# Loading v and k of the first four chunks from ScalarE's DMA queue in a retention kernel with two MLPs

## The chip, the core and the metric

The kernel runs on one core of a Trainium2 chip. TensorE (PE) multiplies matrices, VectorE (DVE), ScalarE (ACT) and GpSimd (POOL) work on elements, and SyncE (SP) issues transfers. A transfer between HBM and SBUF is issued as one instruction by an engine's sequencer and carried out by the core's 16 DMA engines. The metric is the device time of one execution in microseconds (us); lower is better.

## What is computed

A multi-head retention layer (2 sequences, 8 heads, 768 steps, head size 64), then two MLPs of 512 to 2048 to 512 on its 1536 tokens, all in float32.

```python
for t in range(S):
    state = gamma[None, :, None, None] * state + np.einsum('bhd,bhe->bhde', k[:, :, t], v[:, :, t])
    y[:, :, t] = scale * np.einsum('bhd,bhde->bhe', q[:, :, t], state)
x = y, tokens by 512
h = x @ w_in;  x = (h * tanh(log1p(exp(h)))) @ w_out      # first MLP
h = x @ w_in2; out = (h * cos(h)) @ w_out2                # second MLP
```

## The kernel before

The time steps are cut into chunks of 128, so there are 12 chunks (`NCHK`), numbered g = 0 to 11; chunks 0 to 5 are the first sequence, 6 to 11 the second. A chunk's inputs are one array of 128 rows by 2048 float32. Columns 0 to 1023 hold q and k transposed (below "qk"); columns 1024 to 2047 hold v and k in natural order (below "vk"). Each half is one transfer of 512 KB (`att_load`, L281, the issue itself is L294), so the 12 chunks are 24 transfers. `chunk_loads` (L584) plans them, in the order qk0, vk0, qk1, vk1 and so on. Everything is issued on SP: first the constants (`few`, L758, 146 KB), then the chunks, with four halves of weight tiles (`raw`, L211) among them.

What is done with a chunk, in the order in which PE meets it (`chunk_scores`, `chunk_inter`, `chunk_update`, `chunk_out`):

- scores (L325, below "s"), which need qk; DVE multiplies them by a mask (L332, tile `p`)
- inter (L370, "i"), which needs the state of the chunk before (tile `st`, from ACT at L353 or DVE) and `qd`, q times a decay, made by POOL from qk (L313, L316); not for chunks 0 and 6
- update (L341, "u"), which needs vk and `vd`, v times a decay, made from vk by ACT for chunks 1, 2, 4, 7 and 9 (L308) and by POOL for chunks 0, 3, 6, 8 and 10 (L305); not for chunks 5 and 11
- out (L381, "y"), which needs `p` and vk; ACT (L395) and DVE (L398) then store the result as x in a high and a low part

PE's order is s0, some multiplications of zeros (L787), s1, u0, y0, s2, i1, u1, y1, s3, i2, u2, y2, and so on: the scores of a chunk always stand ahead of the rest of the chunk before. After chunk 11 the two MLPs run as float32 products split in three terms (L428 and L451), for the remaining 525 us.

The order of the instructions comes from `Plan`: every step is entered with an engine, an estimated cost and what it needs, a list scheduler sets one order of all steps, and they are recorded in that order. Each engine runs its own in that order and waits on semaphores for the others. Transfers take eight semaphores (DMAHW0 to DMAHW7) in turn, in recorded order; a transfer whose semaphore was used by an earlier one is issued only after that earlier one has landed. So at most eight transfers are under way at a time.

Of the kernel before, what the change touches and what calls it, by code (L numbers as in the profile page):

```python
# [31 lines left out]
NCHK = B * NCH  # L32
IN_WO = (5, 6, 7)
IN_G = (8, 9)
H_ATT = {(0, 0, 0): "s", (0, 1, 0): "h0", (0, 0, 1): "y", (0, 1, 1): "h0"}
VD_ACT = (1, 2, 4, 7, 9)
ST_ACT = (3, 4, 6, 7, 8, 9)
# [34 lines left out]
class Plan:  # L72
# [15 lines left out]
    def op(self, engine, cost, fn, *args, needs=(), uses=(), new=None):  # L88
        n = len(self.ops)
        uses = list(uses)  # L90
        before = set(needs)
        reuse = None
        if new is not None:
            key, bufs, *tag = new
            line = self.lines.setdefault(tag[0] if tag else key[0], [])
            if line:
                before.add(self.owner[line[-1]])
            if len(line) >= bufs:
                reuse = line[-bufs]
            line.append(key)  # L100
            self.owner[key] = n
            uses.append(key)
        for key in uses:
            if self.owner.get(key, n) != n:
                before.add(self.owner[key])
            self.users.setdefault(key, set()).add(n)
        if engine in self.given:
            before |= {self.last[engine]} if engine in self.last else set()
            self.last[engine] = n
        att = fn.__name__.startswith("att") or fn.__name__ in ("start_up", "zeros", "load_consts")  # L110
        self.ops.append(dict(engine=engine, cost=cost, fn=fn, args=args, before=before, reuse=reuse, att=att))
        return n
# [64 lines left out]
def retention_two_mlps(ctx: ExitStack, tc: tile.TileContext, qkv, w1i, w1o, w2i, w2o, consts, out):  # L177
    nc = tc.nc
# [14 lines left out]
    spare = const_p.tile([128, 1], F32, name="spare")  # L193
# [87 lines left out]
    def att_load(g, lo, hi, eng=nc.sync):  # L281
        if not att:
            t = x_p.tile([128, 2, KD, BLK], F32R, tag="x", name="qkv")
            for n in range(2):
                att[n] = t[:, n].rearrange("p a b -> p (a b)").bitcast(F32)
        elif g in IN_WO and g not in att:
            t = wo_p.tile([128, 2, 2, 512], F32R, tag="wo", name="qkv")
            att[g] = t.rearrange("p a b c -> p (a b c)").bitcast(F32)
        elif g in IN_G and g not in att:
            t = g_p.tile([128, 2, 2, BLK], F32R, tag="g", name="qkv")  # L290
            att[g] = t.rearrange("p a b c -> p (a b c)").bitcast(F32)
        elif g not in att:
            att[g] = att_p.tile([128, 2048], F32, tag="qkv", name="qkv", bufs=3)
        eng.dma_start(out=att[g][:, lo:hi], in_=qkv[g, :, lo:hi])  # L294
# [117 lines left out]
    def h_tag(k):  # L412
        if k in H_ATT:
            return H_ATT[k]
        return "h0" if k[0] == 0 and k[1] < 2 else f"h{1 - k[2]}"
# [115 lines left out]
    plan = Plan()  # L531
    op = plan.op
    at = {"gs": []}
# [47 lines left out]
    def chunk(g):  # L581
        return ("qkv", max(g, 1))

    def chunk_loads(g, cuts, queue=nc.sync):  # L584
        key = chunk(g)
        for lo, hi in zip(cuts, cuts[1:]):
            n = op(
                "SP", (hi - lo) * (0.00142 if g < 3 else 0.00122), att_load, g, lo, hi, queue,
                uses=[key], new=None if key in plan.owner else (key, 3, "x" if g < 2 else "wo" if g in IN_WO else "g" if g in IN_G else "qkv"),
            )  # L590
            for part, last in (("qk", 1024), ("v", 1536), ("k", 2048)):
                if lo < last and hi > last - 512:
                    at.setdefault((part, g), []).append(n)

    def chunk_pre(g):
        c = g % NCH
        key = chunk(g)
        on_act = g in VD_ACT
        if c + 1 < NCH:
            at["vd", g] = [  # L600
                op(
                    *(("ACT", 0.98) if on_act else ("POOL", 1.15)), att_vd, g, part, needs=at["v", g] + at["dec"],
                    new=None if part else (("vd", g), 2), uses=[key, ("vd", g)],
                )
                for part in range(2 if on_act else 1)
            ]
        if c > 0:
            name, cost, eng = ("DVE", 0.72, nc.vector) if g in QD_DVE else ("POOL", 1.95, nc.gpsimd)
            at["qd", g] = op(
                name, cost, att_qd, g, eng, needs=at["qk", g] + at["decq"], new=(("qd", g), 2), uses=[key]  # L610
            )

    def nothing():
        pass
# [42 lines left out]
    def tile_in(m, G, j, f, parts=range(KD), only=None):  # L657
# [9 lines left out]
        for kks, terms in calls:  # L667
# [5 lines left out]
            )  # L673
            if H_ATT.get(k, "h0") != "h0":
                plan.ops[last]["att"] = True
# [12 lines left out]
        elif m == 0:  # L688
            last = op("ACT", 1.06, mish, k, needs=[last, table], new=(t, 3), uses=[h])
            plan.ops[last]["att"] = H_ATT.get(k, "h0") != "h0"  # L690
        else:
# [68 lines left out]
    def few(lo, n):  # L760
        return few_t[0][:, lo : lo + n]
# [34 lines left out]
    at["close"] = op(None, 0.0, close)  # L796
    op("PE", 5.5, start_up)
    load = op("SP", 0.4, load_consts, new=("few", 3, "g"))
    cuts = (0, 1024, 2048)
    for g in range(7):  # L800
        chunk_loads(g, cuts)
    weight(("i", 0, 0), lambda: [chunk_loads(g, cuts) for g in (7, 8, 9)])
    for g in (10, 11):
        chunk_loads(g, cuts)
# [16 lines left out]
    def products(n):  # L821
        for i, f, *rest in deal.get(n, ()):
            tile_in(*steps[i], f, *rest)

    chunk_pre(0)
    chunk_scores(0)
    op("PE", 1.1, zeros, 10, "u")
    for n in range(NCHK):
        if n + 1 < NCHK:
            chunk_pre(n + 1)  # L830
            chunk_scores(n + 1)
        chunk_inter(n)
        chunk_update(n)
        chunk_out(n)
        products(n)
        for it in later.get(n, ()):
            weight(it)
    def hold(n, *first):
        plan.ops[n]["before"] |= set(first)

    i00, i01 = ("i", 0, 0), ("i", 0, 1)
    for n, what, ns, it in (
        (6, "clamp", 0, i00), (7, "sign", 0, i00), (11, "dve low", 0, i00),
        (9, "clamp", 1, i00), (11, "dve low", 1, i00),
    ):
        hold(at[what, it, ns], at["p", n])
    hold(at["sign", i00, 1], at["xl", 9])
    hold(at["act", i00, 0], at["xh", 4])
    hold(at["act", i00, 1], at["xh", 6])
    hold(at["high", i00, 1], at["st", 10])  # L850
# [84 lines left out]
```

## Time and profile before

| what | value |
|---|---|
| median of 3 runs | 572.44 us |
| lowest and highest | 571.8 and 572.52 us |
| the profiled execution's own time | 573.28 us |
| its span, first to last instruction | 571.5 us |
| PE busy | 565.8 us, 99% of the span |
| granted PE clock | full throughout the span |
| bytes moved by transfers | 49.91 MB |

The span is the stretch that the trace shows; 1.8 us of the profiled execution lie around it. Times below count from the span's start. A row of the timeline gives start, length, engine, line, operation, output and input tiles, and in square brackets how long the engine had been idle and what released it. PEld is PE's weight load, SPq the sequencer of SP.

### The profile page before, as it was taken

What the parts mean: (1) busy time and instruction counts of PE and PEld (TensorE: products, weight loads), DVE (VectorE), ACT (ScalarE), POOL (GpSimd) and SP (SyncE); (2) the same over time, 40 slices, a digit from 0 to 9 for tenths busy, and PEclk for the clock granted to TensorE, in tenths of its full rate; (3) what the DMA queues carried; (4) which work ended last, traced back from release to release, by engine and by line L of the source; (5) the groups of instructions that cost most, each with busy time, mean ns of one, the idle gap of its engine ahead of it and who ended that gap; (6) DMA issues with size and microseconds to landing.
All of it is one profiled execution on the core that took longest, in us unless ns stands there. A gap on an engine that the chain in (4) does not pass through costs nothing.

```text
span 571.5 us, 7260 instructions
## 1 busy us (share of the span) xinstructions
PE 565.8 (99%) x3054; PEld 468.4 (82%) x3054; DVE 382.6 (67%) x416; ACT 230.1 (40%) x284; POOL 97.5 (17%) x74
## 2 busy tenths in 40 slices
PE   8999999999999999999999999999999999999997
PEld 6888888888888888888888888888888888888886
DVE  5779889662375427653487985898498894765462
ACT  3574543422303303214326465465345354354240
POOL 6680001111110301111101111032010312010000
PEclk9999999999999999999999999999999999999999
DMA  8982254422032200412021030304004010000113
GB/s 297 413 335 75 75 210 158 147 75 73 1 131 91 73 1 0 148 73 75 0 75 73 26 123 1 138 10 147 1 0 148 32 41 2 1 1 1 73 38 110
DMA packets 14721, 49.91 MB, mean 87 GB/s; under 512 B 1632, under 2 KB 2016, under 8 KB 14688
## 3 DMA queue, kind: packets, MB, share of 16 engines
q1 hardware_dynamic: 14688, 49.44, 23.4%
q8 instruction: 24, 0.39, 0.3%
q14 instruction: 9, 0.07, 0.0%
HBM read 46.29 MB, written 3.15 MB: 86 GB/s over the span
## 4 chain that ended last, share of the span: by engine, by line
PE 94%; DMA 4%; SPq 1%; ACT 0%; issue 0%; DVE 0%; ACTq 0%
PE ps_h L428 46%; PE ps_o L451 46%; DMA qkv<-qkv_dram 4%; SPq L294 1%; PE ps_y L381 1%; PE ps_y L370 1%; PE ps_s L325 1%; PE ps_u L341 0%; ACT vd L308 0%; ACT x L395 0%; DVE acc L517 0%; SPq L758 0%; ACT st L353 0%; ACTq L308 0%
## 5 line engine op out<-in xcount | busy, mean ns | idle before, releaser
L428 PE MATMUL ps_h<-x,wi 128*128 128x512 f32 x1152 | 264.8, 389 | 0.0
L428 PEld LDWEIGHTS ps_h<-x,wi 128*128 128x128 f32 x1152 | 216.1, 188 | 45.0 <-issue 0.2
L451 PE MATMUL ps_o<-wo,g 128*128 128x512 f32 (+1 forms) x588 | 132.5, 385 | 0.0
L451 PE MATMUL ps_o<-g,wo 128*128 128x512 f32 x576 | 132.3, 389 | 0.0
L451 PEld LDWEIGHTS ps_o<-wo,g 128*128 128x128 f32 x588 | 108.9, 188 | 22.1
L451 PEld LDWEIGHTS ps_o<-g,wo 128*128 128x128 f32 x576 | 108.1, 188 | 22.5
L494 DVE TENSOR_TENSOR g<-mish,g 128x1024 fp32r<-128x1024 f32 x24 | 33.4, 1393 | 59.2 <-ACT g L490 59.2
L262 POOL TENSOR_TENSOR wo<-mag,wo 128x1024 fp32r<-128x1024 f32 x14 | 35.8, 2557 | 212.8 <-ACT wo L248 212.8
L510 DVE TENSOR_TENSOR acc<-ps_o,acc 128x1024 f32<-128x1024 f32 x35 | 42.8, 1222 | 34.6 <-PE ps_o L451 34.4
L262 POOL TENSOR_TENSOR wi<-mag,wi 128x1024 fp32r<-128x1024 f32 x12 | 30.3, 2525 | 193.1 <-ACT wi L248 193.1
L461 ACT ACTIVATE mish<-ps_h 128x1024 f32<-128x1024 f32 (+1 forms) x25 | 24.9, 995 | 95.1 <-PE ps_h L428 95.1
L474 DVE SCALAR_TENSOR_TENSOR turns<-whole,turns 128x1024 f32<-128x1024 f32 x24 | 29.4, 1223 | 44.7 <-ACT whole L470 44.7
L466 ACT ACTIVATE turns<-ps_h,quarter 128x1024 f32<-128x1024 f32 x24 | 26.7, 1114 | 65.4 <-PE ps_h L428 65.1
L239 DVE SCALAR_TENSOR_TENSOR mag<-raw,mag 128x1024 uint32<-128x1024 uint32 (+1 forms) x38 | 42.2, 1110 | 1.1
L483 ACT ACTIVATE turns<-turns 128x1024 f32<-128x1024 f32 x24 | 25.5, 1062 | 34.8 <-DVE turns L480 34.6
L494 DVE TENSOR_TENSOR g<-turns,g 128x1024 fp32r<-128x1024 f32 x24 | 33.2, 1384 | 8.0 <-ACT g L490 8.0
L486 DVE TENSOR_TENSOR turns<-turns,ps_h 128x1024 f32<-128x1024 f32 x24 | 29.2, 1216 | 10.1 <-ACT turns L483 6.8
L254 DVE SCALAR_TENSOR_TENSOR mag<-raw,mag 128x1024 uint32<-128x1024 uint32 x26 | 33.7, 1301 | 0.4
L490 ACT CAST g<-turns 128x1024 fp32r<-128x1024 f32 x24 | 25.1, 1044 | 16.9 <-DVE turns L486 16.9
L248 ACT CAST wi<-mag 128x1024 fp32r<-128x1024 f32 (+1 forms) x20 | 17.5, 876 | 27.3 <-DVE mag L254 22.4
L470 ACT ACTIVATE whole<-turns,magic 128x1024 f32<-128x1024 f32 x24 | 27.7, 1153 | 0.8
L480 DVE TENSOR_SCALAR turns<-turns 128x1024 f32<-128x1024 f32 x24 | 27.0, 1126 | 0.8
(50 smaller groups left out, 330.2 us busy)
## 6 DMA issues: line engine op xcount, KB each, us to landing
qkv<-qkv_dram SPq DMA_DIRECT2D x24, 512.0 KB, 10.1
raw<-w1i_dram SPq DMA_DIRECT2D x16, 512.0 KB, 4.2
raw<-w1o_dram SPq DMA_DIRECT2D x16, 512.0 KB, 4.1
raw<-w2i_dram SPq DMA_DIRECT2D x16, 512.0 KB, 4.0
raw<-w2o_dram SPq DMA_DIRECT2D x16, 512.0 KB, 3.6
out_dram<-acc SPq DMA_DIRECT2D x11, 256.0 KB, 2.1
out_dram<-acc SPq DMA_DIRECT2D x2, 128.0 KB, 1.7
few<-consts_dram SPq DMA_DIRECT2D x1, 146.0 KB, 2.2
```

Source lines behind the costliest of these rows:

```text
L239: nc.vector.scalar_tensor_tensor(out=a, in0=high, scalar=0xC0000000, in1=a, op0=ALU.bitwise_and, op1=ALU.bitwise_or)
L254: nc.vector.scalar_tensor_tensor(out=w_all_of(it, single)[:, ns], in0=raw_t[it][:, ns, :, 0], scalar=29, in1=mag_t[it][:, ns], op0=ALU.log ...
L262: eng.tensor_sub(out=w[:, :, 1], in0=w_all_of(it, single)[:, ns].bitcast(F32), in1=w[:, :, 0].bitcast(F32))
L428: nc.tensor.matmul(h[:, 0 if h_tag(k) == "s" else f % 2, :], w[:, f % 2, a, kk * 128 : (kk + 1) * 128], x[:, b, kk, :], start=(a + b + kk ...
L451: nc.tensor.matmul(ps, lhs, rhs, start=(n == 0), stop=(n == 3 * GF - 1))
L466: nc.scalar.activation(out=t_t[k], in_=h_t[k], func=AF.Identity, scale=INV_2PI, bias=quarter)
L470: nc.scalar.activation(out=n_t[k], in_=t_t[k], func=AF.Identity, bias=magic)
L474: nc.vector.scalar_tensor_tensor(out=t, in0=n_t[k], scalar=MAGIC, in1=t, op0=ALU.subtract, op1=ALU.subtract)
L480: nc.vector.tensor_scalar(out=t, in0=t, scalar1=-0.5, scalar2=0.5, op0=ALU.max, op1=ALU.min)
L486: nc.vector.tensor_mul(out=t_t[k], in0=t_t[k], in1=h_t[k])
L494: nc.vector.tensor_sub(out=g[:, :, 1, :], in0=t_t[k], in1=g[:, :, 0, :].bitcast(F32))
L510: nc.vector.tensor_add(out=acc, in0=o_t[m * NG + G, j, p], in1=acc)
```

## The change

`act_loads` is a new step on ACT. It copies one column of the constants into a scratch tile, so that ACT waits for the constants to land, and then issues the vk halves of chunks 0 to 3 from ACT's own queue. In SP's plan the four entries stay, but with `nothing` in place of the load, and whoever needs vk0 to vk3 now needs `act_loads` as well. The `hold` helper only moves up in the file. The transfers' sizes, sources and destinations stay what they were.

```diff
+ON_ACT = (0, 1, 2, 3)
...
-    def chunk_loads(g, cuts, queue=nc.sync):
+    def act_loads():
+        nc.scalar.copy(out=spare, in_=few(0, 1))
+        for g in ON_ACT:
+            att_load(g, 1024, 2048, nc.scalar)
+
+    def chunk_loads(g, cuts):
         key = chunk(g)
         for lo, hi in zip(cuts, cuts[1:]):
+            by_act = g in ON_ACT and lo
             n = op(
-                "SP", (hi - lo) * (0.00142 if g < 3 else 0.00122), att_load, g, lo, hi, queue,
+                "SP", (hi - lo) * (0.00142 if g < 3 else 0.00122), *((nothing,) if by_act else (att_load, g, lo, hi)),
...
+            if by_act:
+                at.setdefault(("v", g), []).append(on_act)
+                at.setdefault(("k", g), []).append(on_act)
...
     load = op("SP", 0.4, load_consts, new=("few", 3, "g"))
+    on_act = op("ACT", 0.3, act_loads, needs=[load], uses=["few"])
```

On PE, DVE and POOL the same instructions stand in the same order as before. On SP and ACT the start differs. In the rows, `qkv_129` is the tile that holds chunks 0 and 1; `qkv_178`, `qkv_222` and `qkv_270` are chunks 2, 3 and 4 before, and `qkv_151`, `qkv_153` and `qkv_271` the same chunks in the changed kernel. "waits DMAHW1_49" names the semaphore of an earlier transfer.

SP at the start of the program, before:

```order
L758 DMA few_127<-consts_dram 128x292
L294 DMA qkv_129<-qkv_dram 128x1024 x4
L294 DMA qkv_178<-qkv_dram 128x1024 x2
L294 DMA qkv_222<-qkv_dram 128x1024
L294 DMA qkv_222<-qkv_dram 128x1024 [waits DMAHW0_49]
L294 DMA qkv_270<-qkv_dram 128x1024 [waits DMAHW1_49]
L294 DMA qkv_270<-qkv_dram 128x1024 [waits DMAHW2_49]
L294 DMA qkv_314<-qkv_dram 128x1024 [waits DMAHW3_49]
```

SP at the same place, changed:

```order
L771 DMA few_127<-consts_dram 128x292
L295 DMA qkv_129<-qkv_dram 128x1024 x2
L295 DMA qkv_151<-qkv_dram 128x1024
L295 DMA qkv_153<-qkv_dram 128x1024
L295 DMA qkv_271<-qkv_dram 128x1024 [waits DMAHW1_49]
L295 DMA qkv_271<-qkv_dram 128x1024 [waits DMAHW2_49]
L295 DMA qkv_315<-qkv_dram 128x1024 [waits DMAHW3_49]
L295 DMA qkv_315<-qkv_dram 128x1024 [waits DMAHW4_49]
```

The first four qkv transfers of SP are now qk0 to qk3, and the fifth, qk4, waits for qk0 to land, as it did before; the semaphores DMAHW3, 5, 6 and 0 are now those of vk0 to vk3.

ACT at the start of the program, before:

```order
L793 ACT_TABLE_LOAD
L793 ACTIVATE spare_85<-quarter_82 128x1 [waits DVE_49]
L308 ACTIVATE vd_206<-qkv_129,cst_92 128x64 [waits DMAHW4_49,Pool_49]
L308 ACTIVATE vd_206<-qkv_129,cst_92 128x64 x7
L395 CAST x_244<-ps_y_211 128x2x2x128 [waits PE_49]
```

ACT at the same place, changed:

```order
L806 ACT_TABLE_LOAD
L806 ACTIVATE spare_85<-quarter_82 128x1 [waits DVE_49]
L586 COPY spare_85<-few_127 128x1 [waits DMAHW0_49,Activation_49]
L295 DMA qkv_129<-qkv_dram 128x1024 x2
L295 DMA qkv_151<-qkv_dram 128x1024
L295 DMA qkv_153<-qkv_dram 128x1024
L309 ACTIVATE vd_209<-qkv_129,cst_92 128x64 [waits DMAHW5_49,Pool_49]
```

The copy, which waits for the constants, and the four transfers vk0 to vk3 stand ahead of ACT's first work on a chunk; the rest of ACT's order is unchanged.

## Rows read from the trace of the kernel before

**Rows 1.** The page: busy time of each engine; chain's shares by engine.

```profile
PE 565.8 (99%) x3054; PEld 468.4 (82%) x3054; DVE 382.6 (67%) x416; ACT 230.1 (40%) x284; POOL 97.5 (17%) x74
PE 94%; DMA 4%; SPq 1%; ACT 0%; issue 0%; DVE 0%; ACTq 0%
```

**Rows 2.** The chain that ended last, 0 to 46 us: start, length, what.

```profile
1.16 0.42 SPq L294
...
6.84 10.58 DMA qkv<-qkv_dram
...
17.44 11.76 DMA qkv<-qkv_dram
...
32.07 0.99 PE ps_y L370 x16
```

**Rows 3.** Stretches: busy of each engine (instructions), granted clock, DMA share, GB/s.

```profile
2.00:6.00 4.00, 4.00 (x21) 2.65 (x18) 2.72 (x9) 0.31 (x2) 2.42 (x9) 1.00 0.93 265
6.00:11.00 5.00, 3.83 (x50) 3.02 (x50) 2.33 (x4) 0.00 (x0) 3.57 (x4) 1.00 1.00 359
11.00:17.00 6.00, 5.92 (x120) 5.09 (x122) 4.54 (x9) 5.08 (x18) 5.01 (x8) 1.00 1.03 416
```

**Rows 4.** The timeline, 3 to 15 us: who starts when which transfer lands.

```profile
3.00 0.17 DVE L764 COPY cst<-few 128x8 f32<-128x8 f32 x1 [2.06 <-DMA few<-consts_dram]
...
6.18 0.97 PEld L325 LDWEIGHTS ps_s<-qkv 64*128 64x128 f32 x16 [0.38 <-DMA qkv<-qkv_dram]
...
8.47 1.04 POOL L305 TENSOR_TENSOR vd<-qkv,cst 128x512 f32<-128x512 f32 x1 [1.03 <-DMA qkv<-qkv_dram]
9.73 0.97 PEld L325 LDWEIGHTS ps_s<-qkv 64*128 64x128 f32 x16 [1.45 <-DMA qkv<-qkv_dram]
...
10.63 1.52 POOL L316 TENSOR_TENSOR qd<-qkv,cst 64x256 f32<-64x256 f32 x2
...
11.04 2.02 ACT L308 ACTIVATE vd<-qkv,cst 128x64 f32<-128x64 f32 x8 [8.72 <-DMA qkv<-qkv_dram]
...
12.46 0.97 PEld L325 LDWEIGHTS ps_s<-qkv 64*128 64x128 f32 x16 [0.32 <-DMA qkv<-qkv_dram]
...
14.15 0.55 PEld L341 LDWEIGHTS ps_u<-vd,qkv 128*64 128x64 f32 x16 [0.17 <-ACT vd L308]
```

**Rows 5.** The timeline of PE inside one chunk, 17.8 to 20.6 us.

```profile
17.85 1.04 PE L381 MATMUL ps_y<-p,qkv 128*64 128x128 f32 x16
...
18.82 1.16 PE L325 MATMUL ps_s<-qkv 64*128 64x128 f32 x16
...
19.91 0.67 PE L370 MATMUL ps_y<-qd,st 64*64 64x128 f32 x16
```

**Rows 6.** The timeline of PE and ACT around chunks 5 to 8, 26 to 33 us.

```profile
26.87 1.09 PE L381 MATMUL ps_y<-p,qkv 128*64 128x128 f32 x16
...
28.05 1.16 PE L325 MATMUL ps_s<-qkv 64*128 64x128 f32 x16
...
29.28 1.06 ACT L308 ACTIVATE vd<-qkv,cst 128x64 f32<-128x64 f32 x4 [1.93 <-DMA qkv<-qkv_dram]
...
30.63 1.16 PE L325 MATMUL ps_s<-qkv 64*128 64x128 f32 x16
...
31.68 0.90 ACT L353 ACTIVATE st<-ps_u,cst 128x64 f32<-128x64 f32 x4
...
32.07 0.99 PE L370 MATMUL ps_y<-qd,st 64*64 64x128 f32 x16 [0.28 <-ACT st L353]
```

**Rows 7.** DMA queues from 14 to 16 us: packets, MB, share; last, us to landing.

```profile
q8 instruction: 1, 0.02, 2.7%
...
qkv<-qkv_dram SPq DMA_DIRECT2D x1, 512.0 KB, 11.7
```

**Rows 8.** SP's issues from 19.9 to 23.4 us; each waited for an earlier landing.

```profile
19.98 0.33 SPq L294 DMA_DIRECT2D qkv<-qkv_dram  x1
...
22.97 0.33 SPq L294 DMA_DIRECT2D qkv<-qkv_dram  x1
```

More of the change, by code (lines that the diff above doesn't have):

```diff
@@ L611, in chunk_pre, with hold @@
             )
+    def hold(n, *first):
+        plan.ops[n]["before"] |= set(first)
     def nothing():
@@ L837, in retention_two_mlps @@
             weight(it)
-    def hold(n, *first):
-        plan.ops[n]["before"] |= set(first)
     i00, i01 = ("i", 0, 0), ("i", 0, 1)
```

## The prediction, made before the changed kernel ran

> **What bounds the kernel now.** I read the page first. PE is busy 99% of the span and makes up 94% of the chain that ended last; transfers make up 4% [rows 1]. So whatever changes in the first 46 us reaches the end only if it moves the moment from which PE never waits again. The chain in order of time shows that moment: nearly all of 6.84 to 29.19 us is transfers (two stretches of 10.58 and 11.76 us), a short piece on ACT follows, and from 32.07 us, the inter product of chunk 7 (i7), it is PE without a break [rows 2]. The question is what the change does to i7.
>
> Two things lead to i7. The first is the stream of transfers. From 11 us on the DMA engines are busy all the time at 416 GB/s [rows 3], or 524,288 bytes / 416 GB/s = 1.26 us per half chunk. vk7 lands at about 29.2 us, when ACT starts vd7; two groups of four of these and a cast later, at 31.68, ACT makes the state that i7 waits for [rows 6]. The second is PE itself. From s2 at 12.46 [rows 4] it hardly stops: it is busy 5.92 of the 6.00 us from 11 to 17 [rows 3]. Inside a chunk an out product takes 0.97 us (17.85 to 18.82) and scores 1.09 (18.82 to 19.91) [rows 5]. Against these, PE's slack toward the stream shows in two places. y5 starts at 26.87 and s7 at 28.05, 1.18 later where 0.97 would do: 0.21 waiting for qk7. s8 starts at 30.63 and i7 at 32.07, 1.44 later where 1.09 would do: 0.35 waiting for the state [rows 6]. So PE may run 0.56 us later from s2 on at no cost, and cannot gain more than 0.56 us unless the stream gets faster too.
>
> **The change part by part.** *What SP loses.* Four issues of about 0.42 us [rows 2]. SP issues far ahead of the engines (a transfer issued between 14 and 16 us landed 11.7 us later [rows 7]), so these 1.7 us are worth nothing. Each later issue still waits for one of the last eight transfers to land, and about as many stay under way; I cost this at nothing, because the queue of about 8 transfers of 1.26 us covers it. If that cover were gone, each transfer that came late would cost its lateness at vk7.
>
> *What ACT gains.* One copy of a column, four issues. The constants have landed at about 3.0 us, when DVE reads them [rows 4]. A copy of 128 x 8 took DVE 0.17 us [rows 4], so ACT issues from about 3.25 us; four times 0.42 us ends at 4.9. ACT has nothing else to do until 11.04 us, having been idle for 8.72 us [rows 4], so even issues at the pace of the transfers, 1.26 us each, would end at 8.3 and be hidden. Cost nothing.
>
> *What moves: when each half lands.* In the trace the order is qk0 (s0 starts at 6.18), vk0 (POOL at 8.47), qk1 (s1 at 9.73), vk1 (ACT at 11.04), qk2 (s2 at 12.46) [rows 4]. An issue at 1.16 us [rows 2] moved its first bytes soon after 2 us, so ACT's transfers move from about 4.3 us. No row shows two queues of data together, so I bound it. At one end ACT's transfers are served at once, and the order is that of before: 0. At the other end they wait for the four of SP: vk0 then lands where the fifth transfer landed before, at 12.4 us. POOL has vd0 (1.04 us) ahead of qd1, which ended at 10.63 + 1.52 = 12.15, 2.4 us after qk1 landed [rows 4]. So i1 starts at 12.4 + 0.1 + 1.04 + 2.4 + 0.1 = 16.0 in place of 12.46 + 1.09 = 13.55. That is 2.45 late; less the slack of 0.56, 1.9 us. The nearest row lies by the first end: an instruction fetch on another queue, q8, took 2.7% of 16 engines x 2 us = 0.9 us in a stretch where a transfer of the data queue needed 11.7 us to land [rows 7]. So a second queue is not put behind what the first has waiting.
>
> I take equal shares. From about 4.3 us vk0 moves beside what is left of qk0 and beside qk1. If qk0 were all moved by then, qk1 and vk0 would both land when the later of the two did before, at 9.7; qk2 and vk1 both at 12.4; qk3 and vk2 two transfers later, at 14.9. s1 and s2 then start as before; vd0 is ready at 10.8, in time for u0 after s1, and qd1 at 13.25, in time for i1. What is late is vd1: vk1 lands 1.4 us later, ACT needs 2.02 us from 12.5, and u1 starts at 14.6 in place of 14.15 [rows 4], 0.45 late. If a part r of qk0 is left at 4.3 us, s2 is r x 1.26 us late instead. Between 2 and 4.3 us, 265 GB/s [rows 3] moved 0.61 MB, of which 0.15 are constants, so 0.46 of qk0's 0.52 MB, and r is 0.1 on the average; a lagging engine may have 0.6, which makes 0.76. So PE is 0.45 to 0.76 us late from chunk 1 or 2 on, and behind 0.56 us of slack 0 to 0.2 us remain at i7. From qk4 on SP's queue is alone again, after the same bytes, so vk7 lands as before.
>
> The Trainium skill ("DMA: Bandwidth & Descriptors", Queues, rings and completion order) says that each DMA engine takes turns between the queues that have work, packet by packet. No run here shows that yet for two data queues; by it the sum is the equal shares' 0 to 0.2 us.
>
> *Sum.* SP 0, ACT 0, order of landings +0.1, stream 0. From the profiled execution's 573.28 us that is 573.4; it lies 0.84 above the median of 572.44, so against the medians I say 572.5.
>
> **The rivals.** *The change does not show at all*: ACT's transfers fit in where they were. 572.4. For it: the same bytes, the same engines.
>
> *Slower, ACT's queue is served late.* This is the far end above: vk0 behind the four qk, POOL's vd0 ahead of qd1, i1 2.45 late, 572.44 + 1.9 = 574.3. Since i1 starts 3.6 us after vk0 lands, it begins to cost when vk0 lands after 13.55 + 0.56 - 3.6 = 10.5, and exceeds 0.2% (1.14 us) after 11.7. Against it speaks q8's quick service; for it, that SP's four are issued first. PE would also stand idle longer ahead of u0; the granted clock stayed at full speed over the gap of 1.17 us before s1 (1.00 in all of [rows 3]), and no row tells what a longer gap does.
>
> *Slower, a second stall of the stream.* Landings are 1.3 us apart, but SP's issues at 19.98 and 22.97 [rows 8], each released by a landing, are 2.99 apart: the stream lost 1.7 us there, and vk7 with it. If the other order makes a second one before vk7, 1.7 us come on top: 574.1. If it makes this one vanish, the gain ends at PE's slack: 571.9.
>
> *Faster, the start of the stream improves.* From 2 to 6 us it moves 265 GB/s, from 6 to 11 us 359, later 416 [rows 3]. If a second queue kept the engines full from 4.3 us, it would win 1.7 x (1 - 265/416) + 5 x (1 - 359/416) = 0.6 + 0.7 = 1.3 us for vk7, and qk2 and with it PE would come about as much earlier: 571.1. For it: the poor rate while SP issues. Against it: the engines are already busy 93% and 100% of those stretches [rows 3], so packets are slow, not missing.
>
> By a rule of the Trainium skill this last rival is worth nothing: "DMA: Bandwidth & Descriptors", Issuing engines are not separate DMA queues, says that issuing from several engines only saves the time of issue. The trace has this time at 0.42 us against 1.26 us of moving, hidden.
>
> **How the numbers follow.** A measurement of this kernel tells about 0.2% (1.14 us) from no change. Equal shares 0.52 (all within 0.2%); no effect 0.12 (within); ACT's queue late 0.14, of which 0.13 slower by more than 0.2%; a second stall 0.08, 0.06 slower, 0.02 the stall gone, within; faster start 0.14, of which 0.11 by more than 0.2%. Faster 0.11, same 0.70, slower 0.19. The likeliest is 572.5. The range takes in most of the faster start (571.2) and most of the late queue (574.1).
>
> **What would show it.** Right: ACT's vk0 to vk3 issued at 3.3 to 5 us; POOL's vd0 starting at 9 to 9.8 instead of 8.47; vd1 at about 12.5; u1 at 14.4 to 15; the transfers at 415 GB/s from 11 us; vd7 at 29.3 and i7 at 32.1 to 32.3. Wrong: vd0 after 10.5 with qd1 and i1 behind it (late queue), vd7 at 28 with s2 before 12 (faster start), or vd7 at 31 (second stall). A granted clock below full speed before 46 us would undo all of it.

## The result

| | before | after |
|---|---|---|
| median of 6 executions | 572.21 us | 576.59 us |
| lowest and highest | 571.63 and 572.54 us | 574.52 and 577.27 us |
| profiled execution: time, span | 573.28, 571.5 us | 575.97, 574.2 us |

The profiled execution of before is not one of its six; that of after is. After is slower by a factor of 1.007, with a 95% interval from 1.0048 to 1.0091. The prediction was 572.5 us, about no change, with a range from 571.2 to 574.1: wrong in the time and in the direction.

Six executions of after fall into three groups. Two took 574.52 and 574.65 us at a mean granted clock of 1.000; the profiled one took 575.97 at 0.997; three took 577.21 to 577.27 at 0.994. So there are two losses: about 2.3 us that every execution has, and 0, 1.4 or 2.7 us that go with the clock. The profile below, of the execution at 0.997, shows both.

**The page of after**, the lines that answer to [rows 1], and the two data queues (packets, MB, share of the 16 engines):

```profile
PE 566.6 (99%) x3054; PEld 469.5 (82%) x3054; DVE 382.8 (67%) x416; ACT 230.4 (40%) x285; POOL 97.3 (17%) x74
...
q1 hardware_dynamic: 14112, 47.34, 22.5%
q10 hardware_dynamic: 576, 2.10, 0.9%
...
PE 97%; issue 1%; POOL 1%; DMA 0%; DVE 0%; POOLq 0%
```

SP's queue is q1, and ACT's four transfers did get a queue of their own, q10. The chain has changed: in [rows 1] 4% of it was transfers, now 0%. PE no longer waits for the stream at the end of the first 46 us; something earlier holds it back for good.

**The timeline of after** (columns as in [rows 4]), 3 to 17 us, then i7 and the first product of the MLPs:

```profile
3.03 2.91 ACTq L295 DMA_DIRECT2D qkv<-qkv_dram  x4
...
6.55 1.16 PE L326 MATMUL ps_s<-qkv 64*128 64x128 f32 x16 [0.38 <-DMA qkv<-qkv_dram]
...
8.86 1.16 PE L326 MATMUL ps_s<-qkv 64*128 64x128 f32 x16
...
11.96 1.04 POOL L306 TENSOR_TENSOR vd<-qkv,cst 128x512 f32<-128x512 f32 x1 [4.58 <-DMA qkv<-qkv_dram]
...
13.06 1.12 PE L342 MATMUL ps_u<-vd,qkv 128*64 128x64 f32 x16 [3.04 <-POOL vd L306]
...
13.96 1.92 PE L382 MATMUL ps_y<-p,qkv 128*64 128x128 f32 x16
...
15.81 1.31 PE L326 MATMUL ps_s<-qkv 64*128 64x128 f32 x16
...
17.06 0.67 PE L371 MATMUL ps_y<-qd,st 64*64 64x128 f32 x16
...
35.07 0.67 PE L371 MATMUL ps_y<-qd,st 64*64 64x128 f32 x16
...
48.32 1.88 PE L429 MATMUL ps_h<-x,wi 128*128 128x512 f32 x7
```

s0 and s1 start at 6.55 and 8.86, against 6.18 and 9.73 in [rows 4]. Then POOL waits 4.58 us for vk0 and starts vd0 at 11.96 instead of 8.47. PE's next instruction is u0, which needs vd0: PE stands idle for 3.04 us and goes on at 13.06. After that y0 takes 1.92 us where [rows 5] has 1.04 for an out product of the same shape.

**Where ACT's transfers were.** The queues of after in three stretches (packets, MB, share), and the issue at 3.03 us (count, size, us to landing):

```profile
q1 hardware_dynamic: 172, 0.64, 83.7%
...
q1 hardware_dynamic: 144, 0.52, 84.3%
q10 hardware_dynamic: 27, 0.11, 17.9%
...
q10 hardware_dynamic: 112, 0.44, 53.3%
q1 hardware_dynamic: 110, 0.40, 49.0%
...
qkv<-qkv_dram ACTq DMA_DIRECT2D x1, 512.0 KB, 8.9
```

The stretches are 4.5 to 7.5 us (q1 alone), 7.5 to 9 and 9 to 11. ACT had issued from 3.03 us, but in the first stretch q10 did not move one packet. From 9 to 11 us the queues share evenly, 112 packets to 110. vk0 landed 8.9 us after its issue, at 11.9.

**Stretches of after** (columns as in [rows 3]); the last two are PE's pause and what follows it:

```profile
2.00:6.00 4.00, 4.00 (x21) 2.74 (x18) 2.77 (x9) 0.51 (x3) 2.47 (x9) 1.00 0.87 198
6.00:11.00 5.00, 3.65 (x44) 2.84 (x42) 2.89 (x4) 0.00 (x0) 1.39 (x1) 1.00 0.99 370
11.00:17.00 6.00, 3.94 (x48) 3.55 (x48) 1.02 (x2) 2.50 (x10) 4.65 (x7) 0.72 1.03 421
9.95:13.06 3.11, 0.07 (x3) 0.00 (x1) 0.69 (x1) 0.00 (x0) 1.10 (x2) 0.95 1.02 419
12.74:16.18 3.44, 3.12 (x34) 2.79 (x36) 1.02 (x2) 1.68 (x7) 3.13 (x6) 0.50 1.02 419
```

Toward the end of PE's 3.04 us without work (0.07 us of the 3.11 in the fourth row were still work) the granted clock fell to half, 1.2 in place of 2.4 GHz, and stayed there for 3.4 us. The transfers run as well as before from 6 us on (370 and 421 GB/s against 359 and 416 in [rows 3]); only the first stretch is poorer, 198 against 265.

**The account.** In every profile of this study the time is the start of the first MLP product (ps_h) plus 527.6 us: 575.97 - 48.32 = 527.65 here. So it is enough to ask when ps_h starts. In after PE never waits again once u0 has begun. An execution with the clock at full speed (that of *only_vk0* below) has 33.85 us from u0 to ps_h without a wait; here it is 48.32 - 13.06 = 35.26, so the half clock cost 1.41 us. Without it the time would be 13.06 + 33.85 + 527.63 = 574.54, which is what the two executions at clock 1.000 took (574.52 and 574.65). Before started u0 right behind s1, at 9.73 + 1.09 = 10.82 [rows 4, 5]. Its ps_h started 573.28 - 527.63 = 45.65, 34.83 later, so 0.98 us of waits stood in between. From the profile of before to that of after u0 is 2.24 later, 0.98 of waits are gone, and the clock adds 1.41, together 2.67; measured 2.69.

### The profile page after: what moved, and what is told of

Its sections match the earlier page's. It is cut to its first block, busy times and chain, and to the rows that moved or that the text cites. A ratio compares the mean times of both kernels' runs of the same rounds, so it can differ in the third digit from the quotient of the medians.

```text
span 574.2 us, 7261 instructions
## 1 busy us (share of the span) xinstructions
PE 566.6 (99%) x3054; PEld 469.5 (82%) x3054; DVE 382.8 (67%) x416; ACT 230.4 (40%) x285; POOL 97.3 (17%) x74
## 4 chain that ended last, share of the span: by engine, by line
PE 97%; issue 1%; POOL 1%; DMA 0%; DVE 0%; POOLq 0%
PE ps_h L429 46%; PE ps_o L452 46%; PE ps_y L382 2%; PE ps_s L326 2%; PE ps_u L342 1%; PE ps_y L371 1%; POOL cst L780 1%; DMA few<-consts_dram 0%; POOL vd L306 0%; DVE acc L518 0%; POOL cst L793 0%; POOL cst L777 0%; POOLq L314 0%
## 5 line engine op out<-in xcount | busy, mean ns | idle before, releaser
L487 DVE TENSOR_TENSOR turns<-turns,ps_h 128x1024 f32<-128x1024 f32 x24 | 29.2, 1216 | 10.1 <-ACT turns L484 6.8
```

What stands on the lines that cost most here:

```text
L487: nc.vector.tensor_mul(out=t_t[k], in0=t_t[k], in1=h_t[k])
```

## Experiments

Each experiment is compared with executions of before on the same chip; their medians are 572.48 us for the first four below, 572.25 for the next four (bridge2, vk0_on_sp, late_order, sp_one), 572.18 for the last three.

| kernel | median us | lowest, highest | ratio to before |
|---|---|---|---|
| only_vk0 | 576.22 | 574.2, 576.37 | 1.0064 [1.0047, 1.0081] |
| act_first | 574.62 | 574.5, 575.91 | 1.004 [1.0027, 1.0053] |
| consts_act | 574.53 | 572.9, 575.07 | 1.003 [1.0019, 1.0041] |
| bridge | 576.77 | 576.51, 578.31 | 1.0079 [1.0061, 1.0096] |
| bridge2 | 574.94 | 574.68, 575.13 | 1.0047 [1.0033, 1.0062] |
| vk0_on_sp | 572.09 | 571.32, 572.83 | 1.000 [0.999, 1.001] |
| late_order | 576.9 | 575.06, 577.48 | 1.0077 [1.0058, 1.0095] |
| sp_one | 575.07 | 574.49, 575.82 | 1.0051 [1.0036, 1.0066] |
| sp_two | 571.85 | 571.61, 572.99 | 0.9995 [0.9986, 1.0004] |
| consts_alone | 573.13 | 572.78, 574.03 | 1.002 [1.001, 1.0029] |
| steady_act | 574.0 | 573.8, 574.64 | 1.0033 [1.002, 1.0046] |

**Which of the four transfers costs the time: only_vk0 and vk0_on_sp.** Two edits of after, one each.

```diff
-ON_ACT = (0, 1, 2, 3)
+ON_ACT = (0,)
...
-ON_ACT = (0, 1, 2, 3)
+ON_ACT = (1, 2, 3)
```

> The changed kernel with vk0 alone on ACT's queue; vk1 to vk3 go back to SP. Theory Q (a transfer on ACT's queue starts moving only after those that SP issued before it; ahead of vk0 now stand qk0, qk1, vk1 and qk2, each a 512 KB transfer): vk0's first packets still come at 7 us or later; with nothing else on ACT's queue it then gets half of the engines, and vd0 starts between 9.5 and 12 us; the time is 573 to 575 us. Theory L (ACT's queue needs some 4.4 us from its first issue to its first packet, whatever SP does): first packet at about 7.5 us too, the same time. Rival C (it is the number of issues from ACT that slows all packets between 3 and 7.5 us): first packets at about 5.5 us, vd0 before 9 us, 572.2 us.

> The changed kernel with vk0 back on SP, so ACT issues vk1, vk2 and vk3 alone. Theory (the loss sits in vk0, which POOL's vd0, u0 and qd1 wait for): vd0 starts by 9 us, PE's idle before u0 is gone, the clock stays full; ACT's first packet still comes at 7 us or later, vk1 lands at about 12 us, u1 is late by less than PE's slack, and the time is 572.2 to 573.2 us. Rival (the second queue spoils the stream itself, whoever uses it): 574 us or more.

With vk0 alone on ACT the loss is there, 576.22 us; with vk1 to vk3 on ACT and vk0 back on SP it is gone, 572.09. The timeline of only_vk0, then that of vk0_on_sp (u0 and ps_h):

```profile
12.73 0.69 PE L342 MATMUL ps_u<-vd,qkv 128*64 128x64 f32 x16 [3.13 <-POOL vd L306]
...
46.58 3.70 PE L429 MATMUL ps_h<-x,wi 128*128 128x512 f32 x15
```

```profile
9.91 0.69 PE L342 MATMUL ps_u<-vd,qkv 128*64 128x64 f32 x16
...
44.10 6.21 PE L429 MATMUL ps_h<-x,wi 128*128 128x512 f32 x26
```

The profiled execution of only_vk0 ran at full clock: 33.85 us from u0 to ps_h, and 574.2 us in all; its other three, at 0.996, took 576.15 to 576.37, some 2.0 us more, of which no profile was taken. vk1 to vk3 on ACT cost nothing that can be measured. The whole loss is in vk0.

**Is it the second queue or the order in which the halves land: late_order.** Everything on SP as before, but issued qk0, qk1, qk2, qk3, vk0, vk1, vk2, vk3; the order on all other engines is unchanged.

```diff
+    def att_early(g):
+        for n in ((1, 2, 3) if g == 0 else ()):
+            att_load(n, 0, 1024)
+        att_load(g, 1024, 2048)
...
+            if g < 4 and lo:
+                what = (att_early, g)
+            elif 0 < g < 4:
+                what = (nothing,)
```

> The kernel before, all on SP, but in the order qk0, qk1, qk2, qk3, vk0, vk1, vk2, vk3. Theory (it is the order of landing, not the second queue): vk0 lands at about 12.4 us, vd0 starts at 12.5, PE idles some 3.5 us or more ahead of u0, the clock falls to half for one or two stretches of 3.4 us, and the time is 575 to 577.5 us, as with the changed kernel or a little above. Rival (two queues side by side cost something of their own): 573 to 574 us.

The loss is there without a second queue: 576.9 us. The timeline, and the stretch behind the pause:

```profile
12.39 1.04 POOL L305 TENSOR_TENSOR vd<-qkv,cst 128x512 f32<-128x512 f32 x1 [5.04 <-DMA qkv<-qkv_dram]
```

```profile
13.48 1.12 PE L341 MATMUL ps_u<-vd,qkv 128*64 128x64 f32 x16 [3.73 <-POOL vd L305]
```

```profile
11.70:18.60 6.90, 5.12 (x56) 4.56 (x60) 1.27 (x3) 4.26 (x17) 5.35 (x7) 0.51 1.03 416
```

vk0 lands at about 12.3 us, close to the far end of the prediction's bound (12.4), and everything follows as in after: PE pauses 3.73 us, and in this execution the half clock lasts 6.9 us, twice as long as in the profiled execution of after; it took 577.27 us at a mean clock of 0.994. The one execution at 1.000 took 575.06. The kernel late_order loses as much as after, and vk0_on_sp, with a second queue, loses nothing: what the second queue costs is the order of landing it brings about.

**What the clock costs: bridge and bridge2.** 28 products of zeros are put into PE's order between s1 and u0, so that PE is busy while it waits. In bridge the planner counts 3.0 us for them, in bridge2 nothing.

```diff
+        if n == 0:
+            op("PE", 3.0, zeros, 28, "u")
...
+        if n == 0:
+            op("PE", 0.0, zeros, 28, "u")
```

> The changed kernel with 28 multiplications of zeros (about 3.0 us at the full clock) between s1 and u0, so that PE does not stand idle while vk0 is awaited. Theory: the 4.4 us that the change costs are two terms, vk0's lateness (about 2.4 us, in all runs) and stretches of half clock of 3.4 us each (about 1.3 us each, in some runs), the second caused by PE's idle 3.1 us ahead of u0. Then u0 still starts at about 13 us, the granted clock is full all through, and the times draw together at 574.2 to 574.8 us. Rival: the clock falls for another reason, or the half clock costs nothing at the end: then 576 to 577 us as in the changed kernel, with a clock below 1.00.

> The changed kernel with the same 28 multiplications of zeros between s1 and u0, this time entered at no cost, so that every other engine keeps exactly the changed kernel's order (in the run bridge the planned cost had reordered VectorE and ScalarE, and PE then waited 1.67 us for a mask product). Theory: two terms, lateness of vk0 and half clock. The clock stays full, PE is as late as vk0 makes it, and the time is 574.2 to 574.8 us in every run. Rival (half clock costs nothing, or falls for another reason): times spread from 574.5 to 577.3 us again.

bridge does not answer the question: with 3.0 us the planner put the work of DVE and ACT in another order, and PE lost 1.67 us in the scores of chunk 3, waiting for a mask product (first row, of bridge); one of its four executions also ran at 0.997 and took 578.31 us. In bridge2 the other engines keep after's order (rows behind it, POOL's vd0 first):

```profile
19.98 1.16 PE L326 MATMUL ps_s<-qkv 64*128 64x128 f32 x14 [1.67 <-DVE p L333]
```

```profile
11.55 1.04 POOL L306 TENSOR_TENSOR vd<-qkv,cst 128x512 f32<-128x512 f32 x1 [4.13 <-DMA qkv<-qkv_dram]
...
10.82 2.16 PE L800 MATMUL ps_w<-zero 128*128 128x256 bf16 x18
13.09 0.69 PE L342 MATMUL ps_u<-vd,qkv 128*64 128x64 f32 x16
...
25.21 1.21 PE L371 MATMUL ps_y<-qd,st 64*64 64x128 f32 x16
...
47.48 2.79 PE L429 MATMUL ps_h<-x,wi 128*128 128x512 f32 x11
```

u0 starts as late as in after, 13.09, but all four executions ran at 1.000, the median is 574.94 and the spread 0.45 us instead of 2.75. So with work for PE in the gap the clock stayed at full speed in four of four executions and the spread is gone; without it, four of six of after and three of four of only_vk0 lost some of the clock. The 2.7 us that bridge2 still loses are not the price of vk0 alone: in its profile vd0 was ready at 12.59, so the zeros themselves held u0 for some 0.4 us, and one inter product (at 25.21) took 1.21 us where the others take 0.67. The cleaner figure for the lateness of vk0 is that of after's two executions at full clock, 2.3 to 2.4 us; the half clock is the rest of after's median, about 2 us.

**How long ACT's queue waits: sp_one and sp_two.** To let ACT's issue come earlier in the sequence, SP is held after one or two transfers until ACT has issued vk0: ACT copies a column into the tile of a later chunk, which SP's load has to wait for and overwrites.

```diff
+            if g == 0:
+                nc.scalar.copy(out=att[1][:, 0:1], in_=few(0, 1))
...
+            if g == 0:
+                att_tile2()
+                nc.scalar.copy(out=att[2][:, 0:1], in_=few(0, 1))
```

> The changed kernel, but SP holds qk1 to qk3 until ACT has issued vk0 (ACT writes one column of qk1's tile after that issue, so SP's transfer waits for ACT). Theory Q (what SP has already handed over goes first): ahead of vk0 stands qk0 alone, ACT's first packet comes at 4.3 to 5.5 us in place of 7.6, vk0 lands at 7.5 to 9 us, PE does not idle for 3 us before u0, the clock stays full, and the time is 572 to 573.2 us. Rival (a transfer on ACT's queue needs its 4.4 us while SP's queue is busy, however little is queued): first packet after 7 us, 574 us or more.

> Between the changed kernel and sp_one: SP hands over the constants, qk0 and qk1 and holds qk2 and qk3 until ACT has issued vk0. Theory Q (at the start, transfers begin in the order in which they were handed over, over both queues; with qk0 ahead ACT's first packet came at 4.2 us, with qk0 to qk2 ahead at 7.6): the first packet comes at 5.5 to 6.5 us, vk0 lands at 9 to 10.5 us, qk1 at about 8.5 and qk2, now behind vk0, at 12 to 13 us; PE idles less than 2 us before u0, the clock stays full, the time is 572.5 to 574 us. Rival (a threshold, not an order: any second queue waits until two 512 KB transfers have moved): first packet at 7.4 us or later, vk0 lands at 11.5, time as the changed kernel's.

sp_one, 4 to 6 us (queues), and its timeline; then the timeline of sp_two:

```profile
q10 hardware_dynamic: 94, 0.38, 78.5%
q1 hardware_dynamic: 40, 0.12, 15.3%
```

```profile
10.80 1.94 PE L326 MATMUL ps_s<-qkv 64*128 64x128 f32 x16 [3.03 <-DMA qkv<-qkv_dram]
```

```profile
9.01 1.04 POOL L306 TENSOR_TENSOR vd<-qkv,cst 128x512 f32<-128x512 f32 x1 [1.57 <-DMA qkv<-qkv_dram]
...
10.11 0.69 PE L342 MATMUL ps_u<-vd,qkv 128*64 128x64 f32 x16 [0.57 <-POOL vd L306]
```

With only qk0 ahead of it, ACT's queue has most of the traffic from 4 to 6 us. But now SP's qk1, handed over behind ACT's, is the late one: s1 starts at 10.80 instead of 9.73, after a pause of 3.03 us, with half the clock behind it (575.07 us, all four executions at 0.997). With qk0 and qk1 ahead, qk1 is in time, vk0 lands at about 9.0 us, PE waits 0.57 us ahead of u0, and the time is that of before. So in these kernels what counts is which transfers are handed over ahead of vk0 and which behind it, not which engine issues it. ACT's first packets came at 4.0 us in sp_one, at 6.0 in sp_two and after 7.5 in after: the more stood ahead, the later.

**Is ACT's queue slow to start: act_first and consts_act.** In act_first ACT issues vk0 to vk3 at its very start, without waiting for the constants. In consts_act all chunks are on SP, as before, and ACT issues the constants.

```diff
-        nc.scalar.copy(out=spare, in_=few(0, 1))
...
+        act_loads()
...
-        nc.sync.dma_start(out=t[:, 0:292], in_=consts[:, 0:292])
+        nc.scalar.dma_start(out=t[:, 0:292], in_=consts[:, 0:292])
```

> The changed kernel, but ACT issues vk0 to vk3 as its very first instructions, without waiting for the constants. Theory Q: with nothing ahead of them the four start moving at about 2 us beside the constants and qk0; vk0 and qk0 both land at 7 to 8.5 us, vd0 starts at 8 to 9 us in place of 11.96, and the time is 572 to 573 us (s0 and s1 somewhat late). Theory L: first packet on ACT's queue at 5 us or later, vd0 at 9.5 us or later.

> The kernel before, with the constants alone issued from ACT's queue as ACT's first instruction, all chunks on SP. Theory L (slow start of ACT's queue): the constants land at 5 to 7 us in place of 3.0, DVE's and POOL's tables are made 2 to 4 us later, and the time is 573 to 576 us. Theory Q (order of issue): the constants are issued at 0.74 us as before with nothing ahead of them and land at 2.7 to 3.1 us; qk0 is issued 0.4 us earlier; the time is 571.8 to 572.3 us.

act_first, then consts_act:

```profile
8.06 1.40 PE L326 MATMUL ps_s<-qkv 64*128 64x128 f32 x16 [2.13 <-DMA qkv<-qkv_dram]
```

```profile
5.57 0.17 DVE L764 COPY cst<-few 128x8 f32<-128x8 f32 x1 [4.63 <-DMA few<-consts_dram]
...
10.39 1.18 PE L325 MATMUL ps_s<-qkv 64*128 64x128 f32 x14 [1.90 <-DVE p L332]
```

The queue is not slow to start: in act_first it moved 94 packets between 2 and 4 us. Issued from the start, the two queues share, and now the constants and qk0 come late: s0 starts at 8.06, and PE's pause of 2.13 us ahead of it is followed by half the clock from 8.9 to 12.2 us (574.62, no execution at full clock). consts_act shows the same of the constants: 146 KB that landed at 3.0 us when they stood alone land at 5.6 beside qk0, so POOL's and DVE's tables are late and vd0 and the masks with them. The stream is earlier there; executions at full clock took 572.9 to 573.17, the others, at 0.996 and 0.997, 574.47 to 575.07.

**Can the start be gained another way: consts_alone.** Constants from ACT, SP's first chunk held (by a memset of its tile) until they are well under way.

```diff
+        nc.scalar.dma_start(out=t[:, 0:292], in_=consts[:, 0:292])
...
+        att_tile()
+        nc.vector.memset(att[0][:, 0:512], 0.0)
```

> The kernel before with the constants issued by ACT at 0.74 us and qk0 held on SP until VectorE has cleared half a row of its tile, some 0.6 us later; all chunks on SP. In consts_act (no hold) the constants' 1168-byte packets took turns with qk0's 4096-byte ones and landed at 5.56 us, while the chunks ran 1.7 us ahead. Theory (handing over first means moving first): the constants land at about 3 us again, qk0 at 5.5 to 6.2 us, and the time is 571.3 to 572.4 us. Rival (any overlap costs the constants their turn): they land at 4 us or later and the time is 573 us or more.

The timeline of consts_alone:

```profile
9.06 1.16 PE L328 MATMUL ps_s<-qkv 64*128 64x128 f32 x16
...
12.96 1.16 PE L328 MATMUL ps_s<-qkv 64*128 64x128 f32 x16 [1.24 <-DMA qkv<-qkv_dram]
```

573.13 us, slightly slower than before. The constants land in time, at about 3 us. qk0 starts late (s0 at 6.57 against 6.18), but this is made up: s1 starts at 9.06 against 9.73. Then s2 waits for qk2 until 12.96 (12.46 in [rows 4]), in a stretch in which the queue was poor: 0.55 MB from 9 to 11 us, 0.63 in before. Why qk2 is late is open, and so what makes the median 0.95 us longer is not shown.

**A second queue in the middle of the stream: steady_act.** Before, with vk5 and vk6 issued by ACT right behind vd1 in its order, at 9.80 and 10.22 us, when SP has handed over ten chunk transfers.

```diff
+        if g == 1 and part == 1:
+            for n in (5, 6):
+                att_load(n, 1024, 2048, nc.scalar)
```

> The kernel before, with vk5 and vk6 issued from ACT's queue after its vd1, at about 13.1 us, when SP's queue holds some seven transfers of 512 KB that were handed over earlier. If at all times what was handed over first moves first, ACT's first packet comes at about 20 us and vk5 lands at 22 to 23 us, as before. If the order of handing over rules only at the start and two queues with work take turns otherwise, the first packet comes within 2 us, vk5 lands at 16 to 17.5 us and vk6 by 20, both far too early to be of use, and SP's transfers of that time (qk3, vk3, qk4) land 1 to 2 us late; the time is then 572 to 575 us.

Queues of steady_act, 10 to 13 us, 13 to 14, 14 to 18, and the timeline:

```profile
q1 hardware_dynamic: 310, 1.13, 98.8%
...
q1 hardware_dynamic: 82, 0.31, 77.2%
q10 hardware_dynamic: 19, 0.08, 18.9%
...
q10 hardware_dynamic: 223, 0.85, 52.4%
q1 hardware_dynamic: 224, 0.80, 48.9%
```

```profile
20.34 1.16 PE L328 MATMUL ps_s<-qkv 64*128 64x128 f32 x16 [1.64 <-DMA qkv<-qkv_dram]
```

For more than 3 us after the issue only q1 moves, some 1.3 MB or two and a half transfers; then both share evenly (223 to 224). Five of SP's transfers were waiting at the time of the issue. So a second queue is neither served at once, nor put behind all that was handed over: about two transfers of the first queue went ahead of it, here and in after. That lies between the two cases expected. The loss, 574.0 us, is again one of order as far as this trace shows: qk halves that PE needs now share with vk5 and vk6, which it needs much later, and PE stands idle for 1.64 us ahead of a score product that waits for its half.

## Why the prediction was wrong

*What bounds the kernel, SP and ACT.* Right. PE's last wait set the time, before and after. ACT issued from 3.03 to 5.94 us, at up to 0.88 us each rather than 0.42, and had nothing else to do until 14.5.

*When each half lands: the step that failed.* "I take equal shares" from 4.3 us. Evidence for it was one instruction fetch on q8 [rows 7]. That row tells how long the packet took once it moved; it does not tell when it was asked for, so it could say nothing of a wait ahead of it. In fact q10 had no packet before 7.5 us; vk0 landed at 11.9, where the two ends were 8.4 and 12.4. A bound with ends 4 us apart should have been decided by what each end does to PE, and the far end was the expensive one. The rule cited beside it (the Trainium skill, "DMA: Bandwidth & Descriptors", Queues, rings and completion order: turns between queues that have work) agrees with this case once both queues move, 112 packets to 110, and not before: a queue whose first transfer had been issued 4.5 us earlier got no turn.

*The late-queue rival* had the kind of cause right: ACT's queue is served late, and vk0 lands behind its threshold (10.5 us). It was not behind all four qk halves, though, but behind about two of them, and shared with the rest. Its chance, 0.14, was far too small. Its price, 574.3, came close to the executions at full clock (574.5 to 574.65) by luck, because its terms were off and cancelled. PE's own order did the harm, not POOL's qd1 behind vd0: u0 stood at the head of PE and started 2.24 us late, where the rival has i1 2.45 late. In only_vk0, at full clock, i1 followed u0 by 2.6 us and started at 15.31, when qd1 had been done since 14.97. PE's slack was 0.98 us in the profiled execution of before, not 0.56: beside the two waits counted, i7 itself took 0.99 us where an undisturbed one takes 0.67 [rows 5, 6], and s2 waited 0.15. Both make the price too high, by 0.21 and 0.42 us. Against that, the profiled execution lay 0.84 above the median, and the prediction took this off after as well. That makes the price too low by 0.84, and 0.84 less the other two are the 0.2 us that it is short. With vk0 at 11.9, where it did land, the rival's own rule gives 1.4 us (11.9 - 10.5) and not the 2.3 measured. In after PE does not wait for the stream, so a stream that is late in one execution does not lengthen it; an execution of vk0_on_sp with u0 at 9.91 and ps_h at 44.10 took 571.73 us. That the 0.84 us were waits of this kind is likely from this, not shown.

*The clock: the term that was left at "no row tells".* The gap ahead of u0 was foreseen for this rival, and the full speed over a gap of 1.17 us was noted, but no price was put on a longer one. In the profiled execution 3.4 us at the lower level cost 1.4 us. The times and mean clocks of the other five fit none (1.000) or two (0.994) such stretches, though they were not profiled. From 574.5 this makes 576 or 577.2: the median of after lies between. The range ended at 574.1, below even the rival's price without the clock.

*The second stall and the stream.* Right: vk7 landed near 28.7 us against 29.2, and no transfer held PE after u0. *The faster start* did not come: 198 GB/s from 2 to 6 us. The Trainium skill's rule cited against it ("DMA: Bandwidth & Descriptors", Issuing engines are not separate DMA queues: several issuers save only time of issue) agrees in that nothing was won, 198 and 370 GB/s against 265 and 359; that a second issuer can lose 4.4 us through the order and the clock behind it is this case's own result.

*What would show it.* The signs named were the right ones: vd0 after 10.5 and a granted clock below full before 46 us.

## What to carry to other kernels

When a load moves to another queue, ask first which transfers will have been handed over before it and what the consumer at the head of its engine's order waits for; do not count on even sharing from the moment of issue. A pause of TensorE has two prices: its length, less the waits that vanish behind it, and what the clock does afterwards, so put a number or a wide bound on the second, too. And a slack read from one execution belongs to that execution: look how far it lies from the median before it is taken off a sum.

## What the runs showed of the hardware beyond that

- A second queue starts late behind a busy one. In after and in steady_act 1.0 and 1.3 MB of the first queue, about two transfers of 512 KB and two and a half, moved between issue and the second queue's first packet (some 4.7 and 3.6 us); with one or two transfers ahead (sp_one, sp_two) it came at 4.0 and 6.0 us, 1.0 and 2.9 us after the issue. Why it is about two was not found.
- In the profiled executions the granted clock fell to half in or behind pauses of PE of 1.9 us (consts_act), 2.1 (act_first) and 3.0 to 3.7 (after, sp_one, late_order), and not with the 3.1 us of only_vk0, the 1.67 of bridge and the 1.64 of steady_act. It fell 1.8 us before PE went on in late_order and about 1 us after that in consts_act. What decides whether it falls, and for how long, in executions of the same kernel stays open.
- A small transfer can lose much by sharing: the 146 KB of constants took until 5.6 us in place of 3.0 when qk0 ran on the other queue (consts_act).
- From 2 to 6 us the transfers are slow in after, 198 GB/s, with the DMA engines busy 87% of the time, and in before at 265 with 93%; the other profiles lie between 206 and 300, none near the 416 of later. The second queue is not needed for it: late_order, all on SP, has 220. Its cause is open.
- No arrangement tried beat the kernel before by more than the measurement can tell; sp_two and vk0_on_sp equal it.
